# Five conversion units of 512 columns instead of eight of 320 for the lower half of w_out, and another order of the first three chunks' steps

## The chip, the cores and the metric

The kernel runs on one core of one Trainium2 chip. The metric is device time in microseconds (us) of one execution; several executions are timed and the median counts. The engines are TensorE (PE in the profile; PEld is its weight load), VectorE (DVE), ScalarE (ACT), GpSimd (POOL) and SyncE (SP, which here only issues DMAs). ACT issues a few DMAs too.

## The reference

The inputs r, k, v, w, a, b have 4 batches, 8 heads, 768 steps and 40 columns. A recurrence runs over the steps, and its output feeds a two-layer network:

```python
for t in range(S):
    y[:, :, t] = einsum('bhd,bhde->bhe', r_t, state)
    Sa = einsum('bhde,bhe->bhd', state, a_t)
    state = state * w_t[:, :, None, :] - einsum('bhd,bhe->bhde', Sa, b_t)
    state = state + einsum('bhd,bhe->bhde', v_t, k_t)
x = y.transpose(0, 2, 1, 3).reshape(3072, 320)
h = x @ w_in                                   # 320 x 2048
out = (0.5 * h * (1 + erf(h / sqrt(2)))) @ w_out   # 2048 x 320
```

The two weight matrices w_in and w_out arrive as 64-bit floats, and the kernel converts them to 32 bits itself.

## The kernel before, in words

**Chunks.** The 768 steps are cut into 12 chunks of 64. Within a chunk the recurrence is written as matrix products. For chunk c the function `logs` takes logarithms of w, `sums` builds running sums of them on PE (tiles `wT_ps` and `cum`) and takes exponentials of these on ACT. `scale_a`, `scale_b` and `scale_k` scale a, b and k by them; `turn_a`, `turn_b`, `turn_k`, `turn_v` and `turn_r` transpose on PE (eight flips of 128x128, tiles `aT_ps`, `nT_ps` and so on) and copy out of PSUM, mostly on ACT. `make_N`, `make_A`, `make_RV` and `make_M` are the products of pairs of these, each masked on DVE at L575. N must be inverted as a triangular matrix. For chunk 0 `squares` does this on PE in repeated steps (tiles `sq`, with copies on POOL, ACT and DVE between them). For later chunks `make_N` writes N to DRAM by SP (L615), `start_inverse` reads it back in another layout (L664) and solves column by column on POOL (L672, L674), `store_inverse` writes the result (L686) and `fetch_inverse` brings it back (L696, L700) as Tt. `turn_corner` transposes a part of it on DVE (tile `L`, L772), and `corner`, `joined` and `make_X` go on from there (tiles `J`, `Js`, `X`). `make_sa` and `make_saT`, `make_QY` and `outputs` end the chunk. `outputs` writes the chunk's rows of x (tile `xt`, L886, and DMAs at L894 and L897) and the next state (`st`, L906 to L909), which `turn_state` flips.

**The network.** `mlp` is a generator for one block of rows: first products `ph` at L993, the Gelu on ACT at L995, second products `po` at L1010. Each `fill()` in the order below emits one more piece of it. The xt buffer that `outputs(1)` writes is free once the `ph` of the first block is done.

**The order.** All engines run their instructions in program order, so the order in which the functions are called is the schedule. For the first three chunks the calls are written out by hand, from L1059 on; from chunk 2 on, a loop follows at L1244. `keep(n)` asks for a filler, a matmul of no use of n times 128 columns, put on PE before the next PSUM tile that `duo` hands out; when two `keep` calls meet before a tile, the last one counts. Three fillers of 512 columns stand at the very start.

**The conversion.** `to_float` converts a unit of columns: on DVE two operations on the words (L319, L321) with one on ACT (L320) after the first, then a `yield`, then three on DVE (L324, L327, L328). A variant that runs partly on POOL (L330 to L333) serves some units of w_in. `convert(1)` begins the next unit in the queue and finishes the one begun before it; `convert(0, True)` finishes what is begun. `first_load` brings raw words of w_in, `first_convert` converts them in units of 512 columns. `second_load(f, slot)` brings the raw words of rows f (128 of the 2048) of w_out by two DMAs (L401). The raw words of f = 0 to 7 lie in w_out's own SBUF memory, `late_raw`, one behind the other; those of f = 8 to 15 lie in memory that is free at the time. LW is 1024 words. `second_convert(f)` converts 320 columns.

```python
    def second_convert(f, eng):
        if wide_out:
            yield from to_float(w_out_sb[:, f], second_raw.pop(f), eng)
```

**Queues.** SP issues most DMAs in the written order, and an issue that must wait (for a landing, or for memory to come free) holds back those behind it. Rows f10 of w_out go into k's memory, so their issue waits for `scale_k(2)`. DMAs issued by ACT stand in ACT's own order of work.

Of the kernel before, what the change touches and what calls it, by code (L numbers as in the profile page):

```python
# [10 lines left out]
FP32 = mybir.dt.float32  # L11
# [8 lines left out]
def kernel(  # L20
# [71 lines left out]
    def keep(columns):  # L92

        asked[:] = [columns]
# [119 lines left out]
    def load_VR(c):  # L214
        VR = turned_in.setdefault(c, {})["VR"] = VR_ring()
        for e in range(2):
            nc.sync.dma_start(out=VR[half(e)].rearrange("p g q m d -> p (g q m) d")[:, :, :D], in_=rows_of(v, c, e))
# [188 lines left out]
    def second_convert(f, eng):  # L406
        if wide_out:
            yield from to_float(w_out_sb[:, f], second_raw.pop(f), eng)

    def first_pieces(kts, part, eng):  # L410
        queue.extend(first_convert(kt, part, eng) for kt in kts)

    def second_pieces(fs, eng):
        queue.extend(second_convert(f, eng) for f in fs)

    def run(steps):
# [6 lines left out]
    def logs(c):  # L423
        logw = raws[c, "w"][:, :G * DM]
        nc.scalar.activation(logw, logw, ACT.Ln)

    def sums(c):
        logw = raws.pop((c, "w"))
        pt = duo("wT_ps").rearrange("p e (n t) -> p e n t", t=C)
        for n in range(G * NP):  # L430
            for x in range(2):
                for e in range(2):
                    at = (2 * n + x) * D
                    mm(pt[half(x), e, n], logw[half(e), at:at + HP], cum_m[half(e), half(e)])
        cum = duo("cum")[:, :, :DM]
        for g in range(G):
            for e in range(1 if c < NB else 2):
                q = half(e ^ g) if c >= NB else slice(0, P)
                mm(cum[half(e) if c >= NB else q, g], cum_m[q, q], logw[q, g * DM:(g + 1) * DM])
        wp = wp_ring()  # L440
        turned_in.setdefault(c, {})["wp"] = wp
        if c < NB:
            nc.scalar.activation(wp[:, :, 1:].rearrange("p (n e) t -> p e n t", e=2), pt, ACT.Exp)  # L443
        else:
            en = turned_in.setdefault(c, {})["en"] = by_batch(side("en", "kT", 1))
            for to, scale_ in ((wp[:, :, 1:].rearrange("p (g n e) t -> p g e n t", g=G, e=2), 1.0),
                               (en.rearrange("p (e g n) t -> p g e n t", e=2, g=G), -1.0)):
                for g in range(G):
                    nc.scalar.activation(to[:, g], pt[:, ::1 - 2 * g, g * NP:(g + 1) * NP], ACT.Exp, scale=scale_)
        rw = (avs_ring if c in (1, 2) else part_ring)()[:, :, :DM]  # L450
        nc.scalar.activation(rw, cum, ACT.Exp, scale=-1.0)
        decays[c] = rw.rearrange("p g (h d) -> p g h d", h=H), wp
# [25 lines left out]
    def turn_a(c):  # L478
        if c < NT:
            turned_in.setdefault(c, {})["a_ps"] = flip(by_pair(raws.pop((c, "a"))), "aT_ps")  # L480
            return
        aT = turned_in.setdefault(c, {})["aT"] = work.tile([P, 2, G, NP, C], FP32, tag="aT", name="aT", bufs=2)
        turn(aT.rearrange("p e g i t -> p (e g i) t"), c, "a")
# [569 lines left out]
    def warm(*columns):  # L1053

        pt = duo("warm")
        for n, cols in enumerate(columns):
            mm(pt[:, n % 2, :cols * P], ident, cum_m.unsqueeze(1).to_broadcast([P, cols, P]))

    logs(0)  # L1059
    keep(4)  # L1060
    keep(1)
    sums(0)
    turn_a(0)
    scale_b(0)
    load_r(0)
    spare_N = work.tile([P, BL * BL], FP32, tag="Nb", name="Nb"), work.tile([P, BL // 2 * BL], FP32, tag="W", name="W")
    turn_b(0)
    load_VR(0)
    nw = BL // 2 * BL
    fetch(0, "k", k, nc.sync)  # L1070
    spare_st = st_ring()
    spare_w = spare_st.rearrange("p e i g d -> p (e i g d)")
    logs(1)
    scale_a(0)
    make_N(0)
    zero = squares(0, spare_w, *spare_N, nc.gpsimd)
    next(zero)
    sums(1)
    scale_b(1)
    turn_a(1)  # L1080
    turn_b(1)
    first_pieces((0,), 0, nc.vector)
    fetch(1, "k", k, nc.sync, ahead["k"])
    spare_x = work.tile([P, NK, TB], FP32, tag="xt", name="spare_x").rearrange("p k t -> p (k t)")
    scale_a(1)
    scale_k(0)
    make_N(1)
    next(zero)
    next(zero)
    next(zero)  # L1090
    run(start_inverse(1, nc.gpsimd, (spare_x[:, :BL * BL], spare_w[:, :nw], spare_w[:, nw:])))
# [12 lines left out]
    corner_direct(0, (nc.scalar, nc.scalar, nc.scalar, nc.scalar))  # L1104
    first_load(False, 1, eng=nc.sync)
    make_av(0)
    make_y2(0)
    turn_k(1)
    make_X(0)
    first_pieces((1, 2), 0, nc.gpsimd)  # L1110
    mask_RV(0)
    first_pieces((3,), 0, nc.vector)
    load_VR(1)
    joined_direct(0)
    load_r(1)
    make_A(1, False)
    convert(1)
    convert(0, True)
    load_a(2)
    make_sa(0)  # L1120
    convert(0, True)
    load_w(2)
    mask_A(1)
    make_saT(0)
    convert(0, True)
    convert(1)
    make_M(0)
    logs(2)
    keep(1)
    make_QY(0)  # L1130
    first_load(False, 2, early(5, 4), eng=nc.sync)
    convert(1)
    fetch(2, "b", b, nc.sync)
    first_pieces((4,), 0, nc.gpsimd)
    store_inverse(1)
    convert(0, True)
    fetch(2, "k", k, nc.sync)
    fetch_inverse(1)
    pieces.append(mlp(0))
    turn_v(1)  # L1140
    convert(1)
    first_load(False, 3, eng=nc.sync)
    outputs(0)
    corner(1)
    keep(2)
    convert(1)
    keep(4)
    first_pieces(range(NK - 1), 1, nc.gpsimd)
    make_av(1)
    first_load(True, 1, spare_raw[:, :LW], eng=nc.sync)  # L1150
    convert(0, True)
    second_load(1, 2, eng=nc.sync)
    keep(3)
    keep(1)
    make_X(1)
    sums(2)
    joined(1)
    turn_r(1)
    scale_b(2)
    spare_rT = words("rT", 2)  # L1160
    turn_state()
    convert(1)
    second_load(0, 0, eng=nc.scalar)
    turn_a(2)
    turn_b(2)
    scale_a(2)
    pieces.append(mlp(1))
    keep(4)
    make_RV(1)
    first_pieces((NK - 1,), 1, nc.vector)  # L1170
    for n in "av": unused(paired[n], nc.gpsimd)
    make_sa(1)
    keep(1)
    convert(1)
    make_N(2)
    convert(1)
    convert(1)
    fill()
    scale_k(2, nc.vector)
    run(start_inverse(2, nc.gpsimd))  # L1180
    make_saT(1)
    convert(1)
    second_load(10, 0, k_rows[0][:, :2 * DM].bitcast(UINT32), eng=nc.sync)
    convert(0, True)
    convert(0, True)
    second_load(7, 14, eng=nc.sync)
    fill()
    second_load(2, 4, eng=nc.sync)
    make_y2(1)
    second_load(4, 8, eng=nc.scalar)  # L1190
    second_load(5, 10, eng=nc.sync)
    second_load(9, 2, spare_raw, eng=nc.sync)
    load_VR(2)
    make_M(1)
    second_load(3, 6, eng=nc.scalar)
    load_r(2)
    second_pieces(range(NF), nc.vector)
    make_QY(1)
    convert(1)
    convert(1)  # L1200
    second_load(6, 12, eng=nc.scalar)
    convert(1)
    second_load(8, 0, spare_raw, eng=nc.sync)
    load_VR(3)
    convert(1)
    turn_k(2)
    second_load(11, 0, spare_rT, eng=nc.scalar)
    convert(1)
    fill()
    fill()  # L1210
    load_a(3)
    load_w(3)
# [1 line left out]
    outputs(1)  # L1214
    turn_r(2)
    turn_v(2)
    convert(1)
    logs(3)
    make_RV(2)
    make_A(2)  # L1220
    convert(1)
    fetch(3, "b", b, nc.sync)
    convert(1)
    sums(3)
    turn_a(3)
    convert(1)
    make_av(2)
    second_load(12, 12, eng=nc.sync)
    store_inverse(2)
    fetch_inverse(2)  # L1230
    convert(1)
    unused(paired["r"], nc.vector)
    convert(1)
    turn_state()
    turn_corner(2)
    convert(1)
    second_load(13, 14, eng=nc.sync)
    scale_b(3)
    scale_a(3)
    fetch(3, "k", k, nc.sync)  # L1240
    fill()
    second_load(15, 0, spare_rT, eng=nc.sync)

    for c in range(2, NCH):  # L1244
        n, n2 = c + 1, c + 2
# [122 lines left out]
```

## Time and profile before

| | |
|---|---|
| median of 6 runs | 713.01 us |
| the six runs | 710.23 to 715.96 us |
| the profiled execution | 711.44 us |
| its span, first to last instruction | 709.7 us |
| mean granted PE clock | 0.959 of full |
| busy over the span | PE 671.0, DVE 368.6, POOL 346.3, ACT 219.5 us |

Busy time is summed per engine. Lines such as L324 are lines of the kernel before. The granted clock is the share of full speed that PE is given; it is 0.5 or 1.0 at any time here, and a mean over a stretch lies between. In a timeline line, the first figure is the start, the second the duration; the bracket at the end gives the idle time of the engine just ahead and what ended it.

### The profile page before, as it was taken

The page shows a single profiled execution, that of the slowest core. Times are in us where ns is not written, and L with a number is a line of the kernel's source. Part 1 is how long each engine was busy: PE and PEld are TensorE (multiplying, and loading weights), DVE is VectorE, ACT ScalarE, POOL GpSimd, SP SyncE. Part 2 cuts the span into 40 slices and gives each one's busy share as a digit, 9 for nine tenths or more (in the row PEclk, how much of TensorE's full clock was granted, in tenths as well). Part 3 has the DMA queues.
Part 4 walks back from the last instruction along what each step waited for, and adds up shares of the span by engine and source line. Part 5 has one row for each costly group of instructions (what it writes and reads, how often), then busy time and mean ns, then how long its engine had stood idle before and what let it go on. Part 6 is the DMA issues. An engine that isn't in the chain of part 4 may idle for free.

```text
span 709.7 us, 32732 instructions
## 1 busy us (share of the span) xinstructions
PE 671.0 (95%) x14778; PEld 588.5 (83%) x14778; DVE 368.6 (52%) x485; ACT 219.5 (31%) x304; POOL 346.3 (49%) x798
## 2 busy tenths in 40 slices
PE   7778897869999999999999999999999999999997
PEld 5667787748877877899899898998998898998987
DVE  2324689994353365365484474572672772522303
ACT  5223665443140240351241332232323413112020
POOL 4375358810851842861853844826816818800000
PEclk9575799999999999999999999999999999999999
DMA  9588637763667657656656747747638563120100
GB/s 130 96 176 146 121 88 201 138 128 89 124 121 114 131 99 108 130 103 110 130 103 118 133 90 133 140 77 142 133 68 159 112 108 61 29 46 4 31 8 19
DMA packets 287923, 74.46 MB, mean 105 GB/s; under 512 B 265736, under 2 KB 284456, under 8 KB 287784
## 3 DMA queue, kind: packets, MB, share of 16 engines
q1 hardware_dynamic: 283360, 68.20, 51.5%
q0 software_dynamic: 864, 2.36, 2.1%
q8 instruction: 116, 1.90, 1.1%
q10 hardware_dynamic: 3560, 1.80, 0.9%
q14 instruction: 23, 0.19, 0.1%
HBM read 58.69 MB, written 9.70 MB: 96 GB/s over the span
## 4 chain that ended last, share of the span: by engine, by line
PE 81%; SPq 6%; DVE 5%; DMA 3%; ACT 2%; issue 2%; ACTq 1%; DVEq 0%
PE ph L993 29%; PE po L946 19%; PE po L1010 7%; PE QY L110 6%; PE J L110 2%; PE X L110 2%; PE av L110 2%; PE wT_ps L110 2%; PE RV_ps L110 2%; SPq L383 2%; PE sap L110 2%; PE N_ps L110 2%; PE saT_ps L110 1%; PE A_ps L110 1%; PE M_ps L110 1%
## 5 line engine op out<-in xcount | busy, mean ns | idle before, releaser
L993 PE MATMUL ph<-xt,w_in_sb 64*128 64x256 f32 x1920 | 219.9, 381 | 0.7 <-issue 0.7
L993 PEld LDWEIGHTS ph<-xt,w_in_sb 64*128 64x128 f32 x1920 | 183.1, 187 | 22.7 <-issue 1.6
L672 POOL TENSOR_TENSOR tmp<-W,Nb 128x126 f32<-128x126 f32 (+22 forms) x310 | 122.3, 394 | 159.9 <-DMA Nb<-N 136.9
L674 POOL TENSOR_TENSOR W<-W,tmp 128x126 f32<-128x126 f32 (+22 forms) x310 | 129.3, 417 | 24.3
L995 ACT ACTIVATE gt<-ph 128x1024 f32<-128x1024 f32 x48 | 49.1, 1023 | 152.0 <-PE ph L993 151.9
L946 PE MATMUL po<-w_out_sb,gt 128*128 128x160 f32 x576 | 82.9, 302 | 0.1
L946 PEld LDWEIGHTS po<-w_out_sb,gt 128*128 128x128 f32 x576 | 78.7, 190 | 2.2 <-DVE gt L966 0.4
L1010 PE MATMUL po<-w_out_sb,gt 128*128 128x320 f32 x192 | 55.3, 445 | 3.0 <-ACT wpT L443 3.0
L1010 PEld LDWEIGHTS po<-w_out_sb,gt 128*128 128x128 f32 x192 | 36.5, 194 | 18.4 <-ACT wpT L443 3.2
L802 DVE COPY Tt<-J 32x512 f32<-32x512 f32 x11 | 7.6, 689 | 57.1 <-ACT Tt L802 57.0
L786 ACT COPY Js<-J 128x256 f32<-128x256 f32 x11 | 4.1, 370 | 94.8 <-PE J L110 94.8
L186 DVE STREAM_TRANSPOSE aT<-a_pairs 128x1024 f32<-128x1024 f32 x9 | 11.2, 1245 | 38.7 <-DMA a_pairs<-in_a_dram 38.7
L998 DVE TENSOR_TENSOR half<-gt 128x1024 f32<-128x1024 f32 x9 | 11.2, 1249 | 34.6 <-ACT gt L995 34.6
L950 DVE TENSOR_TENSOR os<-os,po 128x160 f32<-128x160 f32 x36 | 11.5, 320 | 31.2 <-PE po L946 25.5
L946 PE MATMUL po<-extra,half 128*128 128x160 f32 x176 | 26.1, 303 | 0.0
L320 ACT ACTIVATE conv<-conv,rebias 128x320 uint32<-128x320 uint32 (+1 forms) x26 | 16.2, 625 | 31.1 <-DVE conv L319 29.1
L575 DVE TENSOR_TENSOR SM<-M_ps,upper 128x1024 f32<-128x1024 f32 x12 | 14.6, 1214 | 21.4 <-PE M_ps L110 21.4
L946 PEld LDWEIGHTS po<-extra,half 128*128 128x128 f32 x176 | 24.2, 190 | 0.3
L995 ACT ACT_TABLE_LOAD x10 | 12.8, 1283 | 37.1 <-PE ph L993 37.1
L662 POOL MEMSET W<- 128x512 f32 x10 | 5.3, 529 | 32.9 <-DMA inv<-W 32.9
L886 DVE TENSOR_TENSOR xt<-QY,wpT 128x512 f32<-128x512 f32 x24 | 15.5, 686 | 10.9 <-PE QY L110 10.7
L946 PE MATMUL po<-extra,gt 128*128 128x160 f32 x144 | 21.0, 299 | 0.0
(223 smaller groups left out, 1136.8 us busy)
## 6 DMA issues: line engine op xcount, KB each, us to landing
Nb<-N SPq DMA_DIRECT2D x20, 256.0 KB
VR<-in_v_dram SPq DMA_DIRECT2D x24, 160.0 KB
out_dram<-os SPq DMA_DIRECT2D x48, 80.0 KB
b_rows<-in_b_dram SPq DMA_DIRECT2D x22, 160.0 KB
k_rows<-in_k_dram SPq DMA_DIRECT2D x22, 160.0 KB
N<-N SPq DMA_DIRECT2D x44, 64.0 KB
Tt<-inv SPq DMA_DIRECT2D x44, 64.0 KB
a_pairs<-in_a_dram SPq DMA_DIRECT2D x18, 144.0 KB
```

What stands on the lines that cost most here:

```text
L110: nc.tensor.matmul(o, lhsT, rhs, start=first, stop=True, skip_group_check=True)
L320: nc.scalar.activation(power, power, ACT.Relu, bias=rebias, scale=8.0)
L383: eng.dma_start(out=words[half(x), :n, m:m + 2 * P], in_=whole_rows[:HP, :, m:m + 2 * P])
L575: nc.vector.tensor_tensor(to, pt, upper.unsqueeze(1).to_broadcast([P, 2 * G * NP, C]), ALU.mult)
L672: eng.tensor_tensor(t, W[:, :rows, j:j + 1].to_broadcast([P, rows, rest]), Nb[:, j:j + 1, j + 1:].to_broadcast([P, rows, rest]), ALU.mult)
L674: eng.tensor_tensor(W[:, :rows, j + 1:], W[:, :rows, j + 1:], t, ALU.add)
L886: nc.vector.tensor_tensor(xt[:, :NP, g * P:(g + 1) * P].rearrange("p i (e t) -> p i e t", e=2), Y, wp[:, g, :, :, :C], ALU.mult)
L946: nc.tensor.matmul(po[:, n, :DM // 2], l_[:, f], r_[:, f], start=f == 0, stop=f == NF // 2 - 1)
L950: nc.vector.tensor_tensor(to, one_, other, ALU.add)
L993: nc.tensor.matmul(ph[:, x, s], w_in_sb[half(x), kt, p * P:(p + 1) * P], xt[half(x), kt], start=kt == 0, stop=kt == NK - 1)
L995: nc.scalar.activation(gt[:, 4 * q:4 * q + 4].rearrange("p (x s) t -> p x s t", x=2), ph, ACT.Gelu)
L1010: nc.tensor.matmul(po[:, g], gt[:, f, g * P:(g + 1) * P], w_out_sb[:, f], start=f == 0, stop=f == NF - 1)
```

## The change

It has two parts. In the first, rows f = 0 to 7 of w_out, whose raw words lie one behind the other, are converted by a new function `second_wide(u)` in five units of 512 columns (NK is 5, and one unit covers LW = 1024 raw words), instead of eight of 320; the rows f = 8 to 15 remain units of 320. Unit 0 needs the loads f0 and f1, unit 1 needs f1, f2 and f3, unit 2 f3 and f4, unit 3 f4, f5 and f6, unit 4 f6 and f7. In all there are 13 units instead of 16, and so 65 DVE operations and 13 on ACT instead of 80 and 16. The loads f12 and f13 go into the raw memory of rows 6 and 7, so they now stand behind unit 4.

In the second, the calls of the first three chunks are in another order. On the engines that comes to this. On PE the fillers are 512 columns before nT(0), nT(1), vT(1), av(1) and aT(2) and 128 before sap(1); they were 128 before wT(0) and vT(1), 512 before av(1), 128 before X(1), 512 before RV(1) and 128 before N(2). The flips nT(0) come ahead of aT(0), and A(2) ahead of RV(2). On SP the fetch of k for chunk 1 stands behind the write of N(1); f2, f5 and f4 stand ahead of f10, and f7 after f8; the store of inv(2) stands ahead of f12. f4 goes from ACT's queue to SP, f9 and f15 from SP to ACT's queue (f9 ahead of f3). On DVE the pieces of units stand elsewhere between the masks of chunks 1 and 2, and scale_a(3) comes ahead of scale_b(3). POOL's order stays. The diff (in the changed kernel, lines from L410 on are 5 or 6 higher):

```diff
--- before.py
+++ after.py
@@ -407,10 +407,16 @@
         if wide_out:
             yield from to_float(w_out_sb[:, f], second_raw.pop(f), eng)
 
+    def second_wide(u, eng):
+        if wide_out:
+            at = slice(u * LW // 2, (u + 1) * LW // 2)
+            yield from to_float(w_out_sb.rearrange("p f d -> p (f d)")[:, at], late_raw[:, u * LW:(u + 1) * LW], eng)
+
     def first_pieces(kts, part, eng):
         queue.extend(first_convert(kt, part, eng) for kt in kts)
 
     def second_pieces(fs, eng):
+        queue.extend(second_wide(u, eng) for u in range(NK))
         queue.extend(second_convert(f, eng) for f in fs)
 
     def run(steps):
@@ -1056,36 +1062,36 @@
         for n, cols in enumerate(columns):
             mm(pt[:, n % 2, :cols * P], ident, cum_m.unsqueeze(1).to_broadcast([P, cols, P]))
 
+    nw = BL // 2 * BL
     logs(0)
+    sums(0)
+    spare_N = work.tile([P, BL * BL], FP32, tag="Nb", name="Nb"), work.tile([P, BL // 2 * BL], FP32, tag="W", name="W")
     keep(4)
-    keep(1)
-    sums(0)
-    turn_a(0)
     scale_b(0)
     load_r(0)
-    spare_N = work.tile([P, BL * BL], FP32, tag="Nb", name="Nb"), work.tile([P, BL // 2 * BL], FP32, tag="W", name="W")
+    load_VR(0)
+    fetch(0, "k", k, nc.sync)
     turn_b(0)
-    load_VR(0)
-    nw = BL // 2 * BL
-    fetch(0, "k", k, nc.sync)
+    turn_a(0)
+    scale_a(0)
     spare_st = st_ring()
     spare_w = spare_st.rearrange("p e i g d -> p (e i g d)")
+    zero = squares(0, spare_w, *spare_N, nc.gpsimd)
+    make_N(0)
     logs(1)
-    scale_a(0)
-    make_N(0)
-    zero = squares(0, spare_w, *spare_N, nc.gpsimd)
     next(zero)
     sums(1)
     scale_b(1)
+    first_pieces((0,), 0, nc.vector)
     turn_a(1)
+    keep(4)
     turn_b(1)
-    first_pieces((0,), 0, nc.vector)
-    fetch(1, "k", k, nc.sync, ahead["k"])
     spare_x = work.tile([P, NK, TB], FP32, tag="xt", name="spare_x").rearrange("p k t -> p (k t)")
     scale_a(1)
     scale_k(0)
     make_N(1)
     next(zero)
+    fetch(1, "k", k, nc.sync, ahead["k"])
     next(zero)
     next(zero)
     run(start_inverse(1, nc.gpsimd, (spare_x[:, :BL * BL], spare_w[:, :nw], spare_w[:, nw:])))
@@ -1104,109 +1110,103 @@
     corner_direct(0, (nc.scalar, nc.scalar, nc.scalar, nc.scalar))
     first_load(False, 1, eng=nc.sync)
     make_av(0)
+    turn_k(1)
+    first_pieces((1, 2), 0, nc.gpsimd)
     make_y2(0)
-    turn_k(1)
+    mask_RV(0)
     make_X(0)
-    first_pieces((1, 2), 0, nc.gpsimd)
-    mask_RV(0)
+    load_VR(1)
+    load_r(1)
+    load_a(2)
     first_pieces((3,), 0, nc.vector)
-    load_VR(1)
     joined_direct(0)
-    load_r(1)
     make_A(1, False)
     convert(1)
     convert(0, True)
-    load_a(2)
-    make_sa(0)
     convert(0, True)
     load_w(2)
+    convert(0, True)
     mask_A(1)
+    make_sa(0)
     make_saT(0)
-    convert(0, True)
     convert(1)
     make_M(0)
     logs(2)
-    keep(1)
+    first_load(False, 2, early(5, 4), eng=nc.sync)
+    first_pieces((4,), 0, nc.gpsimd)
     make_QY(0)
-    first_load(False, 2, early(5, 4), eng=nc.sync)
     convert(1)
     fetch(2, "b", b, nc.sync)
-    first_pieces((4,), 0, nc.gpsimd)
     store_inverse(1)
     convert(0, True)
+    keep(4)
     fetch(2, "k", k, nc.sync)
     fetch_inverse(1)
+    convert(1)
+    first_load(False, 3, eng=nc.sync)
+    outputs(0)
+    first_load(True, 1, spare_raw[:, :LW], eng=nc.sync)
     pieces.append(mlp(0))
     turn_v(1)
-    convert(1)
-    first_load(False, 3, eng=nc.sync)
-    outputs(0)
     corner(1)
-    keep(2)
     convert(1)
     keep(4)
     first_pieces(range(NK - 1), 1, nc.gpsimd)
+    convert(0, True)
     make_av(1)
-    first_load(True, 1, spare_raw[:, :LW], eng=nc.sync)
-    convert(0, True)
     second_load(1, 2, eng=nc.sync)
-    keep(3)
-    keep(1)
     make_X(1)
     sums(2)
     joined(1)
+    spare_rT = words("rT", 2)
     turn_r(1)
+    turn_state()
+    keep(4)
     scale_b(2)
-    spare_rT = words("rT", 2)
-    turn_state()
-    convert(1)
-    second_load(0, 0, eng=nc.scalar)
+    convert(1)
     turn_a(2)
+    pieces.append(mlp(1))
     turn_b(2)
     scale_a(2)
-    pieces.append(mlp(1))
-    keep(4)
+    second_load(0, 0, eng=nc.scalar)
     make_RV(1)
     first_pieces((NK - 1,), 1, nc.vector)
+    keep(1)
     for n in "av": unused(paired[n], nc.gpsimd)
     make_sa(1)
-    keep(1)
     convert(1)
     make_N(2)
     convert(1)
+    convert(0, True)
     convert(1)
     fill()
     scale_k(2, nc.vector)
     run(start_inverse(2, nc.gpsimd))
     make_saT(1)
     convert(1)
+    fill()
+    make_y2(1)
+    second_load(2, 4, eng=nc.sync)
+    second_load(5, 10, eng=nc.sync)
+    second_load(4, 8, eng=nc.sync)
     second_load(10, 0, k_rows[0][:, :2 * DM].bitcast(UINT32), eng=nc.sync)
     convert(0, True)
-    convert(0, True)
+    load_VR(2)
+    second_load(9, 2, spare_raw, eng=nc.scalar)
+    second_load(3, 6, eng=nc.scalar)
+    make_M(1)
+    load_r(2)
+    second_pieces(range(NF // 2, NF), nc.vector)
+    make_QY(1)
+    convert(1)
+    second_load(6, 12, eng=nc.scalar)
+    turn_k(2)
+    load_VR(3)
+    second_load(8, 0, spare_raw, eng=nc.sync)
+    convert(1)
+    fill()
+    convert(1)
     second_load(7, 14, eng=nc.sync)
-    fill()
-    second_load(2, 4, eng=nc.sync)
-    make_y2(1)
-    second_load(4, 8, eng=nc.scalar)
-    second_load(5, 10, eng=nc.sync)
-    second_load(9, 2, spare_raw, eng=nc.sync)
-    load_VR(2)
-    make_M(1)
-    second_load(3, 6, eng=nc.scalar)
-    load_r(2)
-    second_pieces(range(NF), nc.vector)
-    make_QY(1)
-    convert(1)
-    convert(1)
-    second_load(6, 12, eng=nc.scalar)
-    convert(1)
-    second_load(8, 0, spare_raw, eng=nc.sync)
-    load_VR(3)
-    convert(1)
-    turn_k(2)
-    second_load(11, 0, spare_rT, eng=nc.scalar)
-    convert(1)
-    fill()
     fill()
     load_a(3)
     load_w(3)
@@ -1214,32 +1214,32 @@
     outputs(1)
     turn_r(2)
     turn_v(2)
-    convert(1)
+    second_load(11, 0, spare_rT, eng=nc.scalar)
     logs(3)
+    make_A(2)
+    convert(1)
+    fetch(3, "b", b, nc.sync)
     make_RV(2)
-    make_A(2)
-    convert(1)
-    fetch(3, "b", b, nc.sync)
-    convert(1)
+    convert(1)
+    unused(paired["r"], nc.vector)
+    store_inverse(2)
     sums(3)
     turn_a(3)
+    second_load(12, 12, eng=nc.sync)
     convert(1)
     make_av(2)
-    second_load(12, 12, eng=nc.sync)
-    store_inverse(2)
     fetch_inverse(2)
     convert(1)
-    unused(paired["r"], nc.vector)
-    convert(1)
+    convert(1)
+    turn_corner(2)
+    convert(1)
+    scale_a(3)
+    second_load(15, 0, spare_rT, eng=nc.scalar)
+    second_load(13, 14, eng=nc.sync)
     turn_state()
-    turn_corner(2)
-    convert(1)
-    second_load(13, 14, eng=nc.sync)
-    scale_b(3)
-    scale_a(3)
     fetch(3, "k", k, nc.sync)
     fill()
-    second_load(15, 0, spare_rT, eng=nc.sync)
+    scale_b(3)
 
     for c in range(2, NCH):
         n, n2 = c + 1, c + 2
```

More of the change, by code (lines that the diff above doesn't have):

```diff
@@ L1128 @@
     logs(2)
-    keep(1)
+    first_load(False, 2, early(5, 4), eng=nc.sync)
+    first_pieces((4,), 0, nc.gpsimd)
     make_QY(0)
-    first_load(False, 2, early(5, 4), eng=nc.sync)
     convert(1)
     fetch(2, "b", b, nc.sync)
-    first_pieces((4,), 0, nc.gpsimd)
     store_inverse(1)
     convert(0, True)
+    keep(4)
     fetch(2, "k", k, nc.sync)
     fetch_inverse(1)
-    pieces.append(mlp(0))
-    turn_v(1)
     convert(1)
@@ L1143 @@
     outputs(0)
+    first_load(True, 1, spare_raw[:, :LW], eng=nc.sync)
+    pieces.append(mlp(0))
+    turn_v(1)
     corner(1)
-    keep(2)
     convert(1)
@@ L1182 @@
     convert(1)
+    fill()
[3 more added lines that the diff above has]
+    second_load(4, 8, eng=nc.sync)
     second_load(10, 0, k_rows[0][:, :2 * DM].bitcast(UINT32), eng=nc.sync)
     convert(0, True)
-    convert(0, True)
-    second_load(7, 14, eng=nc.sync)
-    fill()
-    second_load(2, 4, eng=nc.sync)
-    make_y2(1)
-    second_load(4, 8, eng=nc.scalar)
-    second_load(5, 10, eng=nc.sync)
-    second_load(9, 2, spare_raw, eng=nc.sync)
     load_VR(2)
+    second_load(9, 2, spare_raw, eng=nc.scalar)
+    second_load(3, 6, eng=nc.scalar)
     make_M(1)
-    second_load(3, 6, eng=nc.scalar)
     load_r(2)
-    second_pieces(range(NF), nc.vector)
+    second_pieces(range(NF // 2, NF), nc.vector)
     make_QY(1)
     convert(1)
-    convert(1)
     second_load(6, 12, eng=nc.scalar)
-    convert(1)
+    turn_k(2)
+    load_VR(3)
     second_load(8, 0, spare_raw, eng=nc.sync)
-    load_VR(3)
-    convert(1)
-    turn_k(2)
-    second_load(11, 0, spare_rT, eng=nc.scalar)
     convert(1)
     fill()
+    convert(1)
+    second_load(7, 14, eng=nc.sync)
     fill()
@@ L1216 @@
     turn_v(2)
-    convert(1)
+    second_load(11, 0, spare_rT, eng=nc.scalar)
     logs(3)
-    make_RV(2)
     make_A(2)
@@ L1222 @@
     fetch(3, "b", b, nc.sync)
+    make_RV(2)
     convert(1)
+    unused(paired["r"], nc.vector)
+    store_inverse(2)
     sums(3)
     turn_a(3)
+    second_load(12, 12, eng=nc.sync)
     convert(1)
     make_av(2)
-    second_load(12, 12, eng=nc.sync)
-    store_inverse(2)
     fetch_inverse(2)
     convert(1)
-    unused(paired["r"], nc.vector)
     convert(1)
-    turn_state()
     turn_corner(2)
     convert(1)
+    scale_a(3)
+    second_load(15, 0, spare_rT, eng=nc.scalar)
     second_load(13, 14, eng=nc.sync)
-    scale_b(3)
-    scale_a(3)
+    turn_state()
     fetch(3, "k", k, nc.sync)
     fill()
-    second_load(15, 0, spare_rT, eng=nc.sync)
+    scale_b(3)
     for c in range(2, NCH):
```

## The prediction

> **What bounds the kernel now.** I read the page's forty slices first, then windows by stage, then windows on the grid on which the granted clock changes, then the timeline at three places. In the slices:
> ```profile
> PE   7778897869999999999999999999999999999997
> PEclk9575799999999999999999999999999999999999
> ```
> Each digit is 17.7 us. TensorE (PE) is full from the tenth slice on; in the second to the fifth it runs far below full clock, and in those its busy digits (7, 7, 8, 8) hold work that would be shorter at full clock. The stages (us, then busy time of PE, weight load, DVE, ACT, POOL with counts, clock, DMA share, GB/s):
> ```profile
> 0.00:52.00 52.00, 38.81 (x984) 31.04 (x984) 14.71 (x17) 17.68 (x20) 26.72 (x75) 0.77 0.79 135
> 52.00:79.32 27.32, 22.52 (x660) 20.52 (x664) 13.85 (x20) 12.87 (x20) 13.36 (x31) 0.50 0.83 143
> 98.50:116.60 18.10, 13.68 (x337) 11.81 (x336) 17.47 (x20) 10.59 (x15) 15.47 (x21) 1.00 0.53 142
> 116.60:131.20 14.60, 14.59 (x217) 13.11 (x217) 14.11 (x27) 4.73 (x7) 12.48 (x28) 0.88 0.98 210
> 131.20:152.30 21.10, 14.20 (x326) 11.02 (x324) 20.41 (x41) 12.95 (x17) 12.28 (x32) 1.00 0.63 112
> 164.90:709.70 544.80, 538.09 (x11396) 477.41 (x11392) 264.52 (x325) 145.86 (x204) 258.43 (x608) 1.00 0.52 96
> ```
> After 164.9 PE idles 6.7 us of 544.8 and the diff has no work there: only an earlier start of that stage can shorten it. Until 52 PE waits on chains through other engines, partly at half clock; from 98.5 to 116.6 and from 131.2 to 152.3 DVE is full; between those, PE. The clock changes on a grid of 3.41 us:
> ```profile
> 11.05:14.46 3.41, 1.84 (x50) 1.47 (x52) 1.61 (x2) 1.66 (x2) 0.00 (x0) 1.00 1.16 153
> 21.29:24.70 3.41, 1.50 (x12) 1.05 (x10) 2.49 (x2) 0.75 (x1) 2.21 (x2) 1.00 0.76 118
> 24.70:28.12 3.42, 3.11 (x150) 2.99 (x154) 1.05 (x1) 0.26 (x1) 0.00 (x0) 0.50 0.02 5
> 41.77:45.18 3.41, 2.31 (x84) 2.22 (x85) 1.06 (x2) 1.01 (x1) 2.83 (x8) 1.00 0.49 113
> 62.25:65.66 3.41, 3.41 (x107) 3.02 (x109) 0.34 (x1) 2.20 (x4) 2.17 (x9) 0.50 1.08 231
> 144.17:147.58 3.41, 1.88 (x7) 1.41 (x8) 3.34 (x8) 3.08 (x5) 0.65 (x2) 1.00 1.18 221
> ```
> A full-clock window with 1.84 or 1.50 us of PE work is followed by half clock; one with 1.88 keeps it. The way up is less plain: 62.25 to 65.66 is full and no rise follows.
>
> **Fillers and the front.** Before, the fillers in the front are one of 128 columns at wT(0) and one at vT(1) (0.49 us). After, there are 512-column ones ahead of nT(0), nT(1) and vT(1), each 1.13 us at full clock like the one at av(1). The chain of chunk 1 in the timeline:
> ```profile
> 20.34 0.70 ACT L451 ACTIVATE avs<-cum 128x640 f32<-128x640 f32 x1 [1.37 <-PE cum L110]
> 21.08 1.56 DVE L489 SCALAR_TENSOR_TENSOR extra<-early_b,avs 128x640 f32<-128x640 f32 x1 [3.16 <-ACT avs L451]
> 22.79 1.06 PE L459 MATMUL nT_ps<-ident,extra 128*128 128x128 f32 x8 [1.07 <-DVE extra L489]
> 25.01 1.99 PE L110 MATMUL N_ps<-aT,nT 40*64 40x64 f32 x64 [1.16 <-ACT nT L523]
> ```
> PE waits 1.07 us before nT(1), so a filler of 1.13 costs at most 0.1 there, and lifts 21.29–24.70 from 1.50 to about 2.5 busy, above the 1.88 that kept the clock. Then N(1) takes about 1.16 us, as products of this shape do at full clock, not 1.99; the first squaring 1.2 instead of 2.00, the second (128 products, 3.64) about 1.9: 0.8 + 0.8 + 1.7 = 3.3 us at most, and 1.7 if only the first two lie on the path. The filler at nT(0) falls in PE's wait for scale_b(0) (0.47 us idle ahead of nT(0), 0.21 ahead of aT(0), which now comes second); it makes N(0) up to 0.5 later, and its 1.13 with the flips behind it shift: I put nT(0) at 11.2, aT(0) at 12.1 to 13.1, N(0) at 14.4. In 11.05–14.46 then lie the two flips of 1.06 and 1.07 whole, less the 0.15 of nT(0) that starts ahead: 1.97, for 1.84 now. If that keeps the clock at 14.46, wT(1) (1.98) and cum(1) (2.50) halve too and N(1) starts some 2.7 earlier: 6.1 in all. I take 4, between 1.7 and 6.1, nearer the middle because a margin of 0.09 over 1.88 is thin.
>
> [...]
>
> **Front queues.** fetch(1,"k") (two DMAs, 1.75 us of SP) goes behind N(1)'s write. SP, freed, then waits for N's landing in any case; behind it queues only the issue of the inverse's columns (0.48 us) and the loads of w_in. Its 320 KB may land beside those columns and delay them by 0 to 2 us; the inverse has about 4 us to spare before L(1) at 82.77. Zero, to +0.5.
>
> **Middle.** At vT(1) the filler grows by 0.64, those at X(1) (0.49) and RV(1) go: between -0.3 and +0.5, taken as 0. PE is busy 18.47 of the 19.18 us from 79.32 to 98.50, so none of it is hidden. A filler before sap(1) lies in DVE-bound time. SP before is stuck behind f10 until 110.71; after, f2, f5, f4 are ahead of it, so they land earlier. f3 stays on ACT's queue, behind f9 now: +1 us, landing near 118.9 against 117.96.
>
> **Conversion.** A unit is five DVE operations and one on ACT:
> ```profile
> L324 DVE SCALAR_TENSOR_TENSOR conv<-words,conv 128x320 uint32<-128x320 uint32 x2 | 1.0, 484 | 0.0
> L324 DVE SCALAR_TENSOR_TENSOR conv<-w_out_sb,conv 128x512 uint32<-128x512 uint32 x5 | 3.4, 691 | 3.3 <-ACT conv L320 3.3
> ```
> Each column costs 1.08 ns, the rest is fixed, near 0.14 us. Undisturbed, 320 columns take 0.32 + 0.32 + 0.48 + 0.48 + 0.49 = 2.09; 512 take 0.42 + 0.42 + 0.69 + 0.74 + 0.69 = 2.96. Eight by 2.09 less five by 2.96: 16.7 - 14.8 = 1.9 us of DVE; beside POOL's chain, where L324 averages 638 ns, up to 4. ACT loses 8 × 0.56 - 5 × 0.73 = 0.8. How much counts? Up to 131.2 PE has 14.59 of 14.60 busy, and outputs(1) waits for it:
> ```profile
> 131.26 1.29 DVE L886 TENSOR_TENSOR xt<-QY,wpT 128x512 f32<-128x512 f32 x2 [0.24 <-PE ph L993]
> 152.33 0.71 DVE L772 STREAM_TRANSPOSE L<-Tt 128x512 f32<-128x512 f32 x1
> 153.19 0.74 PE L110 MATMUL J<-L,N 32*32 32x32 f32 x64 [2.92 <-DVE L L772]
> ```
> So units 0 to 2 save nothing by themselves, and their new wait (unit 1 needs f1, f2 and f3) costs nothing: a stall of some 1.5 us for f3 ends unit 2 near 128.2, 3 us before 131.2. Queued behind that wait on DVE are unit 0's finish and outputs(1); beyond 121.8 the stall becomes time. Between outputs(1) and L(2) DVE now does six starts and six finishes of units of 320 (0.32 + 0.32 and 0.48 + 0.48 + 0.49 undisturbed: 12.5 us in all); after, five starts (one of 512) and five finishes (two of 512): 0.84 + 4 × 0.64 + 2 × 2.12 + 3 × 1.45 = 12.0. That is -0.5 undisturbed, -1.0 with the sharing above; the masks, transposes and the clearing of r beside them are the same. L(2) also needs the inverse, whose chain on POOL (113.06 to 144.9) is 31.8 us here against 27.6 for chunk 1, partly from sharing with DVE; fewer DVE operations shorten it by 0 to 1.5, and its store (145.14) no longer queues behind f12's load. I count 0.5 in all. If the inverse is late, L(2) stays where it is and the 0.5 is gone. In scale_a(3), scale_b(3) swapped, scale_b ends 1.2 later, under second products of the first block that keep PE full to 161.1; f15 on ACT's queue delays the state's copy to about 157.5, under the same cover. Gone, these are +1.2 at most.
>
> **Sum.** -4 (front) + 0 (middle) - 0.5 = -4.5. The profiled run took 711.44 with a span of 709.7, 1.6 below the median of 713.01. So 707 on that run's footing, 708.5 as a median.
>
> **Rivals.** *Only the conversion counts* (0.30): the clock falls in the same windows or N(1)'s lead is lost in chunk 0's chain, which shares the same engines. For it: 1.97 against 1.88, and POOL's 26.72 of work before 52. Then -1 to 0: 712.5.
>
> *The rise at 41.77 is lost* (0.20, slower): the work that raised the clock there is chunk 0's 128-wide k flips, which straddle that boundary if the front moves by 1 to 3 us. From 41.77 to 52.0 PE has 2.31 + 3.42 + 1.13 = 6.9 us at full clock, which at half cost 6.9 more; less 3.4 in front: +3.5, 716.5. It decides from the point where the flips end before the boundary and the following windows see only small products, as at 62.25. Against it: a front that is earlier by a whole window also brings the flips into the window before, and the rise with them.
>
> *A late f3 stalls DVE* (0.05, within the range of the others): with f3 landing 5 us later than I put it, unit 1 starts at 124, unit 2 ends near 133.2, outputs(1) and L(2) are 2 us late, and 2 of the front's 4 are gone: about 711.
>
> **Numbers.** The forecast has 0.45, spread over 703.5 to 711 by the front's 1.7 to 6.1 and the middle's bounds; conversion only 0.30; lost rise 0.20; late f3 0.05. 0.5% is 3.6 us, about what a measurement tells from no change: 709.4 and 716.6. Below 709.4 lie 0.36 of the forecast and 0.04 of the second case, whose ends spread by a run or two either way. A lost rise without the gain in front gives 713.0 + 6.9 = 719.9, with it 716.5: 0.15 of its 0.20 lies above 716.6, and 0.05 more comes from a late f3 together with a late inverse. The rest, 0.40, is between. Range 703.5 to 717.
>
> **What would show it.** Right: N(1) ends by 24 at 1.2 us, the granted clock near 1.00 over 14 to 31, L(2) about 4 to 5 before 152.33, and the stage from J(2) on unchanged at 544.8 or so. Wrong: a clock still 0.50 from 24.7; half clock between 41 and 52; unit 1's first step on DVE after 121.8; L(2) waiting for the inverse and not for DVE.

## The result, and the profile after

| | before | changed |
|---|---|---|
| median | 713.06 us (79 runs) | 716.85 us (37 runs) |
| lowest to highest | 707.46 to 721.31 | 712.06 to 721.18 |
| profiled execution, its span | 711.44, 709.7 | 716.72, 715.0 |
| mean granted clock in it | 0.959 | 0.954 |

The ratio is 1.0051, with an interval of 1.0039 to 1.0063: the changed kernel is slower by about half a per cent, some 3.8 us. The forecast was 708.5. The ratios and intervals in this text leave out three runs in a slower state of the chip (one each of e1, e3 and e6 below), while the medians keep them, so that a ratio need not be that of the medians beside it.

I read the profile after in the order of the one before. In the line of the granted clock over forty slices there is less half clock in the front, a little in the seventh slice, and more in the ninth and tenth (143 to 179 us), where before all are 9:

```profile
PEclk9775698978999999999999999999999999999999
```

The stages, cut at the same times as before (us, then busy time of PE, weight load, DVE, ACT, POOL with counts, clock, DMA share, GB/s):

```profile
0.00:52.00 52.00, 36.80 (x984) 28.00 (x984) 14.88 (x17) 17.68 (x20) 24.05 (x69) 0.87 0.81 126
116.60:131.20 14.60, 12.26 (x192) 11.36 (x194) 10.78 (x17) 3.69 (x5) 12.64 (x26) 0.77 0.90 188
131.20:152.30 21.10, 18.75 (x352) 14.64 (x348) 19.21 (x33) 11.64 (x15) 16.09 (x35) 0.92 0.53 104
152.30:164.90 12.60, 7.71 (x138) 5.96 (x139) 9.89 (x22) 2.97 (x5) 0.77 (x3) 0.59 0.69 142
```

Up to 52 us PE does the same 984 instructions in 2 us less busy time, at a mean clock of 0.87 for 0.77. Still nothing behind them is earlier. In the last stretch PE is busy 7.71 of 12.60 us, at a clock of 0.59. The same stretch before, with 10.61 us busy at 0.86:

```profile
152.30:164.90 12.60, 10.61 (x282) 8.39 (x282) 8.81 (x18) 2.39 (x4) 0.00 (x0) 0.86 0.47 112
```

A ledger by landmarks of the two timelines, the start of each step, before and after: N(1) 25.01 and 26.23; L(1) 82.77 and 85.06; L(2) 152.33 and 156.34; N(3) 163.09 and 168.78; the product sap(2) 169.55 and 175.59. So the changed kernel is 2.3 later at L(1), loses 1.7 from there to L(2), 1.7 from L(2) to N(3) and 0.3 to sap(2). From sap(2) to the end it takes 539.4 us against 540.2. That adds up to the 5.3 us between the spans.

The first 2.3 of these can't be put down to the change. Three executions have before's order up to there, before itself and e1 and e6 below: they start L(1) at 82.77, 84.67 and 82.34. Two executions of the changed kernel, this one and e12 below, start it at 85.06 and 81.50. What is left is around L(2). In the timeline there:

```profile
156.34 0.71 DVE L778 STREAM_TRANSPOSE L<-Tt 128x512 f32<-128x512 f32 x1 [1.26 <-DMA Tt<-inv]
157.19 1.08 PE L110 MATMUL J<-L,N 32*32 32x32 f32 x64 [5.26 <-DVE L L778]
158.20 1.95 PE L110 MATMUL X<-st,aT 40*64 40x40 f32 x64
```

Before, DVE was busy right up to L(2); now it has nothing left to do and waits 1.26 us for the inverse (Tt). PE waits 5.26 us for J instead of 2.92, its granted clock is 0.50 from 154.22 on, and X(2) takes 1.95 us; in e9 below, at full clock, it is 1.14.

### The profile page after: what moved, and what is told of

The parts are those of the page before. It is cut to its first block, busy times and chain, and to the rows that moved or that the text cites. A ratio compares the mean times of both kernels' runs of the same rounds, so it can differ in the third digit from the quotient of the medians.

```text
span 715.0 us, 32719 instructions
## 1 busy us (share of the span) xinstructions
PE 673.6 (94%) x14778; PEld 588.9 (82%) x14778; DVE 365.8 (51%) x470; ACT 219.2 (31%) x301; POOL 347.7 (49%) x798
## 3 DMA queue, kind: packets, MB, share of 16 engines
q0 software_dynamic: 864, 2.36, 2.1%
## 4 chain that ended last, share of the span: by engine, by line
PE 81%; POOL 6%; issue 3%; DVE 2%; SPq 2%; DMA 2%; ACT 2%; ACTq 1%; DVEq 0%; POOLq 0%
PE ph L999 28%; PE po L952 19%; PE po L1016 7%; PE QY L110 5%; PE J L110 2%; POOL W L680 2%; POOL tmp L678 2%; PE RV_ps L110 2%; PE sq L110 2%; PE sap L110 2%; PE X L110 2%; PE N_ps L110 2%; PE saT_ps L110 1%; PE av L110 1%; PE A_ps L110 1%
## 5 line engine op out<-in xcount | busy, mean ns | idle before, releaser
L678 POOL TENSOR_TENSOR tmp<-W,Nb 128x126 f32<-128x126 f32 (+22 forms) x310 | 124.5, 402 | 162.6 <-DMA Nb<-N 139.6
L1001 ACT ACTIVATE gt<-ph 128x1024 f32<-128x1024 f32 x48 | 49.1, 1024 | 154.6 <-PE ph L999 154.5
L320 ACT ACTIVATE conv<-conv,rebias 128x512 uint32<-128x512 uint32 (+1 forms) x23 | 15.2, 666 | 25.2 <-DVE conv L319 25.1
```

The lines of the kernel that those rows point to most:

```text
L320: nc.scalar.activation(power, power, ACT.Relu, bias=rebias, scale=8.0)
L678: eng.tensor_tensor(t, W[:, :rows, j:j + 1].to_broadcast([P, rows, rest]), Nb[:, j:j + 1, j + 1:].to_broadcast([P, rows, rest]), ALU.mult)
L1001: nc.scalar.activation(gt[:, 4 * q:4 * q + 4].rearrange("p (x s) t -> p x s t", x=2), ph, ACT.Gelu)
```

## The experiments

There are two theories. **F**, the front: the new order of the front costs time, because PE there waits for its own instruction code, as I read the 2.38 us at cum(1) in which PE is idle and the profile shows no wait. **W**, the width: the longer DVE operations of the wide units hold up POOL, which works on the inverse of chunk 2 at that time, and the inverse is late. In what follows, "chain" is POOL's work on that inverse, from its first to its last column.

**e1_wide_only**: before, with the units of the changed kernel in the old order.

```diff
-    second_pieces(range(NF), nc.vector)
+    second_pieces(range(NF // 2, NF), nc.vector)   # and second_wide for u = 0..4; three convert(1) fewer
```

> The kernel before in its own order, but rows 0 to 7 of w_out converted in five units of 512 (three convert calls fewer). Theory F (front): the loss of the changed kernel comes from the new order of the front, where PE then waits for its own instruction code (2.4 us at cum(1), 2.0 at a squaring); the wide units by themselves save a little: 711.5 to 713, L(2) at 152.3 or up to 1 us earlier. Rival W (wide units): the longer DVE operations disturb POOL's inverse of chunk 2 (34.6 us long in the changed kernel, 31.8 before), L(2) then waits for the inverse and PE falls to half clock: 714.5 to 716, chain on POOL over 33 us.

Measured: 718.5 us against 714.37 for before on the same chip, ratio 1.0032 (1.0001 to 1.0063). Chain 35.2 us, L(2) waits 2.04 us for the inverse. This is what W expects; the ratio makes 2.3 us, and its interval lies only just clear of no change.

**e2_order_only**: the changed order with eight units of 320.

```diff
-        queue.extend(second_wide(u, eng) for u in range(NK))
-    second_pieces(range(NF // 2, NF), nc.vector)
+    second_pieces(range(NF), nc.vector)            # and three convert(1) more
```

> The changed kernel's order, with rows 0 to 7 of w_out in eight units of 320 as before (three more convert calls). Theory F: as slow as the changed kernel, 716 to 718. Rival W: most of the loss is gone, 713 to 714.5, and POOL's chain for chunk 2 is back near 32 us.

Measured: 0.9989 (0.9960 to 1.0018). Chain 31.4 us, no wait for the inverse, PE waits 0.96 us for J. This speaks for W.

**e3_old_front** and **e4_new_front**: the lines from the first `sums(0)` to the start of chunk 1's inverse exchanged: e3 is the changed kernel with the old lines (the diff shows their start), e4 the kernel before with the new ones.

```diff
-    sums(0)
-    keep(4)
-    scale_b(0)
+    keep(4)
+    keep(1)
+    sums(0)
+    turn_a(0)
+    scale_b(0)
...
```

> The changed kernel with the front (from the first sums to the start of chunk 1's inverse) in the order of before, with its fillers; everything behind as changed. Theory F: N(1) at 25.0, squaring and RV(0) 1.5 us earlier than in the changed kernel, L(1) near 82.8 instead of 85.1; 713 to 714.5. Rival W: L(1) earlier, but the later loss (some 3 us between 116 and 165) stays: 715 to 716.

> The kernel before with only the front in the changed order, with its fillers. Theory F: 714.5 to 716.5, L(1) near 85. Rival W: 713 to 714.

Measured: e3 1.0003 (0.9973 to 1.0032), chain 34.5, L(2) waits 1.39; e4 1.0003 (0.9975 to 1.0031), chain 31.9, L(2) waits 1.11. e3 is better than W alone allows, though its trace shows W's wait, and its L(1) is at 85.67, where F had expected 82.8. e4 is better than F allows; and its L(2) waits for the inverse with narrow units and a chain of 31.9, so width is not the only source of that wait. Width isn't everything in the changed kernel, then, and the front alone costs too little to be seen.

By now the effect on POOL could be read from six traces. In the changed kernel, a POOL operation over 108 columns beside two wide DVE operations:

```profile
140.91 0.73 POOL L678 TENSOR_TENSOR tmp<-W,Nb 128x108 f32<-128x108 f32 x1
141.31 0.88 DVE L327 SCALAR_TENSOR_TENSOR conv<-w_out_sb,conv 128x512 f32<-128x512 uint32 x1
141.72 0.73 POOL L680 TENSOR_TENSOR W<-W,tmp 128x108 f32<-128x108 f32 x1
```

The same POOL operation in the kernel before, beside the same line of a unit of 320:

```profile
136.34 0.69 DVE L327 SCALAR_TENSOR_TENSOR conv<-w_out_sb,conv 128x320 f32<-128x320 uint32 x1
136.76 0.53 POOL L672 TENSOR_TENSOR tmp<-W,Nb 128x108 f32<-128x108 f32 x1
```

It takes 0.73 instead of 0.53 us. The next runs add or remove this by itself.

**e5_wide_cut**: the changed kernel, each of L324, L327 and L328 of a wide unit in two halves.

```diff
-        eng.scalar_tensor_tensor(dst, mant_f, 2.0 ** -20, power_f, ALU.mult, ALU.mult)
+        for s in at:    # two slices of 256 columns; L324 and L327 in the same way
+            eng.scalar_tensor_tensor(dst[:, s], mant_f[:, s], 2.0 ** -20, power_f[:, s], ALU.mult, ALU.mult)
```

> The changed kernel, but in the five wide units each of the last three DVE operations (L324, L327, L328) is cut in two halves of 256 columns: 15 more DVE instructions, some 2 us more DVE time in all, the same data and order. Theory W (long DVE operations hold up POOL: in the first four runs and the two profiles before, a POOL operation beside L327 or L328 took 0.13 to 0.15 us more at 320 columns and 0.34 more at 512, and the chain for chunk 2 lasted 31.4 to 31.9 us with narrow units and 34.5 to 35.2 with wide ones): the chain is back to 31 to 32 us, and the time falls to 0.998 to 1.002 of before in spite of more DVE work. Rival D (the loss sits in DVE's own order or in the front): 1.005 to 1.008, the chain no matter.

Measured: 1.0017 (0.9996 to 1.0037). Chain 31.4 us, no wait of L(2) for the inverse. Chain and wait are as W expects. In time, with 15 more DVE instructions, the kernel is below the changed one's 1.0051 (1.0039 to 1.0063); but that was measured at another time, and e12 below gives the changed kernel 1.0022, so the cut is judged by e9 and e10.

**e6_late_chain**: before, and the inverse alone made late.

```diff
-        eng.memset(W, 0.0)
+        for _ in range(1 + extra):    # extra is 6 for chunk 2
+            eng.memset(W, 0.0)
```

> The kernel before, narrow units, with six more clears of W (0.52 us each) on POOL ahead of chunk 2's inverse, which so ends some 3 us later and is otherwise as it was. If the lateness of the inverse is what the wide units cost: 1.002 to 1.005, with L(2) starting on the arrival of the inverse. If the inverse has slack and the wide units cost something else: 0.999 to 1.001.

Measured: 1.0015 (0.9991 to 1.0039), not clear of no change. The 1.002 to 1.005 expected of a costly late inverse was missed. In the trace L(2) waits, but for much less than with the wide units:

```profile
154.33 0.71 DVE L773 STREAM_TRANSPOSE L<-Tt 128x512 f32<-128x512 f32 x1 [0.27 <-DMA Tt<-inv]
155.19 0.74 PE L110 MATMUL J<-L,N 32*32 32x32 f32 x64 [3.83 <-DVE L L773]
```

L(2) waits 0.27 us for the inverse, PE waits 3.83 us for J, and X(2) behind J takes 1.95 us, at half clock.

**e7_a_flips_first** and **e8_a_first_k_early**: e2 with the a flips first and the filler between the flips cut from 512 to 256 columns; e8 has also the fetch of k back in its place.

```diff
+    turn_a(0)
-    keep(4)
+    keep(2)
     scale_b(0)
...
     turn_b(0)
-    turn_a(0)
     scale_a(0)
```

> The changed order with narrow units (as in e2_order_only), but the flips aT(0) again ahead of nT(0), and the filler between them 256 columns instead of 512. Theory F (PE's wait of 2.4 us for its code at cum(1) comes from N(0) starting 0.9 us later, at 14.8): N(0) back at 13.8 to 13.9, the code lands by 16, N(1) at 22.5 to 23.5 instead of 26.2; what reaches the end is -0.5 to -3 us against e2_order_only, so 0.995 to 0.999 of before. Rival (the code is late whatever PE does, or the front is absorbed later): N(1) at 25 to 26, or no change in time, 0.998 to 1.000.

> As e7_a_flips_first, with the fetch of chunk 1's k also back ahead of N(1)'s write. Chain of chunk 1 on POOL starts at 35 to 37 instead of 39.7. If that chain has slack, no difference to e7 (within 0.1%); if it has none, 1 to 2 us less than e7.

Measured: e7 0.9981 (0.9958 to 1.0005), N(1) at 24.62; e8 0.9992 (0.9970 to 1.0015), N(1) at 22.91. The idle time at cum(1) is gone in e7 and 0.22 us in e8. In e7 the clock was at half during cum(1), which took 2.50 us, so N(1) missed the expected 22.5 to 23.5. Neither time is clear of e2's 0.9989. Moving the fetch of k made no difference that can be seen.

The last four were measured together, on one chip. **e9_cut_a_first** is e5 with e7's front, **e10_wide_a_first** the changed kernel with e7's front, **e11_narrow_cut** is e7 with the last three operations of each unit of 320 in halves of 160, and **e12_changed_again** the changed kernel.

> e5_wide_cut (the changed kernel with the last three DVE operations of each wide unit in halves of 256) with the front of e7_a_flips_first. If the wait of DVE for the inverse was the main cost of the change and the front costs 0.1%: 0.997 to 1.000 of before, chain for chunk 2 near 31.5 us, no wait of L(2) for the inverse. If the units still cost something when cut: 1.001 to 1.003.

> The changed kernel, wide units uncut, with only the front of e7_a_flips_first: N(1) near 24.6 instead of 26.2. If the wide units are the main cause, the chain is still 34.5 us or longer, L(2) waits 1 to 2 us for the inverse, and the time is 1.003 to 1.005. If the front's wait for code is the main cause: 1.000 to 1.002.

> e7_a_flips_first with the last three DVE operations of each of the eight units of 320 cut in halves of 160: 24 more DVE instructions, 3.4 us more DVE time by 0.14 us each. If a POOL operation waits longer the longer the DVE operation beside it, it takes about 0.05 us more beside 160 columns (0.14 beside 320, 0.34 beside 512) and the chain is 30 to 31 us; as DVE is then the later of the two at L(2), the time is 0.2 to 0.5% above e7: 1.000 to 1.003. If it is not length that matters, the chain stays at 31.5.

> The changed kernel itself, on the chip and in the call of the three above, for the comparison: 1.004 to 1.006 by every theory; L(2) waits 1 to 2 us for the inverse, PE 5 us for J.

| | ratio to before | interval | median, us | chain, us | L(2) waits for the inverse | PE waits for J |
|---|---|---|---|---|---|---|
| e9 | 0.9976 | 0.9956 to 0.9997 | 711.29 | 31.3 | no | 0.99 |
| e10 | 1.0008 | 0.9989 to 1.0027 | 714.00 | 34.6 | 1.61 | 5.76 |
| e11 | 1.0019 | 0.9996 to 1.0041 | 714.76 | 28.7 | no | 2.84 |
| e12 | 1.0022 | 0.9999 to 1.0045 | 715.39 | 34.7 | 1.21 | 5.19 |

Before, measured with them, had a median of 712.56. e9 beats both kernels: cut units, a flips first, and the rest of the new order. e9 and e10 differ only in the cut, and by 2.7 us in their medians; from the twelve times of each the means differ by 2.1 us, with an interval of about 0.7 to 3.4. This is the cleanest price of the uncut wide units on record. e10 and e12 differ only in the front, by 1.4 us in their medians, which is not clear of nothing. e12 missed what every theory expected: it is less slow here than the changed kernel was over its 37 runs. And e10 splits the expectations: chain and wait are W's, but its time is below the 1.003 that W gives and within what was expected if the front's wait were the main cause. e11 shows the other side of length: the chain is the shortest of all, but DVE has 24 more instructions and is now the late one.

In e9 the same steps as shown above:

```profile
152.89 0.71 DVE L782 STREAM_TRANSPOSE L<-Tt 128x512 f32<-128x512 f32 x1
153.75 0.83 PE L110 MATMUL J<-L,N 32*32 32x32 f32 x64 [0.99 <-DVE L L782]
154.51 1.14 PE L110 MATMUL X<-st,aT 40*64 40x40 f32 x64
```

No wait on L(2), 0.99 us on J, X(2) at full clock. In e11, beside DVE operations of 160 columns (two in one line of the view), the POOL operation over 108 columns:

```profile
133.78 1.03 DVE L330 SCALAR_TENSOR_TENSOR conv<-w_out_sb,conv 128x160 f32<-128x160 uint32 x2
134.23 0.40 POOL L683 TENSOR_TENSOR W<-W,tmp 128x108 f32<-128x108 f32 x1
```

So 0.73 beside 512 columns, 0.53 beside 320, 0.40 beside 160.

## Why the prediction was wrong, point by point

**Two terms of the sum failed.** The forecast was -4 from the front and -0.5 from the conversion; measured was +3.8. The front's 4 us were the larger miss: by e4, which has the new front alone, they are +0.2 us (-1.8 to +2.2). The conversion had the wrong sign, and is what makes the kernel slower and not merely equal: 2.3 us by e1 (0.1 to 4.5), about 2 by e9 and e10.

**The cost of the wide units had the wrong sign.** The working said that "fewer DVE operations shorten" POOL's chain "by 0 to 1.5". It counted operations and not their length. The mean excess of a POOL operation over the same one left alone, beside L327 or L328, is 0.01 us at 160 columns, 0.07 at 256, 0.13 to 0.16 at 320 and 0.33 to 0.36 at 512 (left alone, such an operation takes 0.18 us and 1.88 ns a column, a line through those with nothing beside them). Five wide units so made the chain 34.5 to 35.2 us long in five traces, against 31.3 to 31.9 in seven with units of 320 or cut in 256 (before, e2, e4, e5, e7, e8 and e9): 3 us longer, where I had a gain. The inverse reached L(2) 1.2 to 2.0 us after DVE was ready for it, in all five.

The lines differ too: at 512 columns the excess is 0.33 to 0.36 us beside L327 and L328, 0.21 to 0.23 beside L324, and 0.06 to 0.10 beside L321, which is small but not nothing. Whether that goes with their inputs in SBUF, two in L324, L327 and L328 and one in L321, was not tried. The trace of before already spoke against the change: at 114.23 a POOL operation over 30 columns takes 0.56 us beside the L327 of a unit of w_in, 512 columns wide, which is 0.33 above the line for one left alone. The prediction, which names the sharing, did not weigh it by length.

**What a late inverse costs comes through the clock.** Between L(2) and N(3) lie 11.9 to 12.6 us in the seven traces in which L(2) waits for the inverse (the changed kernel twice, e1, e3, e10, e4 and e6), and 9.15 to 10.85 in the other seven. That this is the clock is read from X(2): 1.95 us in six of the seven (1.65 in e4), 1.14 to 1.53 in the others. In the changed kernel the granted clock is 0.50 from 154.22 to 164.46, in before from 154.40 to 157.82. In the seven, PE waits 3.5 to 5.8 us for J, in the others 0.96 to 3.74. So the stretch gets up to 3 us longer. That does not always reach the end: e4 and e6 have narrow units and the same 12.4 us from L(2) to N(3), with waits of L(2) of 1.11 and 0.27 us, and their times, 1.0003 and 1.0015, are not clear of no change. The runs don't show why.

**The front's 4 us were not there.** In the first window the clock did what that step said. This is the window that the prediction put at 1.97, and the one after the gain:

```profile
11.05:14.46 3.41, 1.94 (x16) 1.73 (x16) 1.22 (x2) 1.98 (x2) 0.00 (x0) 1.00 1.46 154
17.88:21.29 3.41, 1.57 (x9) 1.29 (x10) 0.62 (x1) 0.56 (x2) 3.18 (x4) 0.97 0.92 121
```

Behind the window with 1.94 busy the clock stayed full: it was 1.00 in 14.46 to 17.88, wT(1) took 1.14 us instead of 1.98, and then PE stopped in cum(1):

```profile
19.71 1.07 PE L110 MATMUL cum<-SM,cum_m 128*128 128x320 f32 x3 [2.38 <-issue]
21.87 1.91 PE L110 MATMUL nT_ps<-cum_m,ident 128*128 128x512 f32 x2
23.57 1.50 PE L465 MATMUL nT_ps<-ident,extra 128*128 128x128 f32 x8
26.23 1.16 PE L110 MATMUL N_ps<-aT,nT 40*64 40x64 f32 x64 [1.16 <-ACT nT L529]
```

"issue" is idle time for which the profile shows no wait. The transfers of the instruction queue suggest what it was: a block of 16,384 bytes ran from 16.49 to 18.07, and PE went on 1.6 us after it. In before that block had landed by 15.76, and PE, at half clock, came to the place at 17.8. So my reading is that a faster PE ran into the end of its code. That the block holds PE's code is inferred: the trace doesn't name its engine, but in all nine traces with idle time at this place (0.22 to 2.71 us) PE goes on 1.5 to 1.75 us after the block has landed. The same wait, 2.3 to 2.7 us, is in all five traces with this front, and 1.38 in e6, whose old front happened to run at full clock. The window with the wait had 1.57 us busy, the clock behind it was 0.53 (21.29 to 24.70), and the filler meant for PE's idle time ran at half clock, 1.91 us. So the front's term left out a wait that in these traces PE meets only when it is faster.

Nor is the border that the prediction drew, between 1.84 and 1.88 us of work, a border. In e1 a full-clock window with 1.62 keeps the clock, in e3 one with 2.36 is followed by half clock:

```profile
20.93:24.35 3.42, 1.62 (x13) 1.18 (x11) 2.88 (x2) 0.34 (x2) 2.03 (x2) 1.00 0.94 156
24.35:27.76 3.41, 1.81 (x124) 1.64 (x128) 1.23 (x1) 0.68 (x1) 0.61 (x1) 1.00 0.02 5
137.67:141.08 3.41, 2.36 (x130) 2.05 (x128) 2.51 (x5) 3.02 (x4) 2.86 (x8) 1.00 0.56 152
141.08:144.49 3.41, 3.34 (x67) 2.83 (x68) 3.38 (x5) 0.63 (x2) 3.02 (x6) 0.50 0.14 30
```

So the margin of 0.09, on which the 4 us rested, was none; what decides is open.

With the a flips ahead of nT(0), N(0) starts at 13.2 to 13.8 (e7 to e11) instead of 13.8 to 14.8, and the wait is 0.8 us or less; the trace of e10:

```profile
17.40 1.07 PE L110 MATMUL cum<-SM,cum_m 128*128 128x320 f32 x3 [0.31 <-issue]
22.91 1.16 PE L110 MATMUL N_ps<-aT,nT 40*64 40x64 f32 x64 [1.16 <-ACT nT L529]
```

But the earlier N(1) does not reach the end: L(1) is at 82.10 in e10 and at 81.50 in e12, whose N(1) is 2 us later. Over all traces L(1) is at 82.3 to 85.7 with the old front (four), 81.5 to 85.5 with the changed one (five) and 81.3 to 83.7 with the a flips first (five). Where between them the lead is lost was not followed. Taking away most of this wait is worth 1.4 us in the medians (e12 less e10), which is not clear of nothing. The second case of the prediction had said as much ("N(1)'s lead is lost in chunk 0's chain").

**The stall before unit 1 was as forecast, what followed it was not.** Unit 1 began at 121.09 after a wait of 1.44 us for its load, within the 121.8 I had set. But unit 2 did not end near 128.2: it ended at 134.0, as the conversions then waited 1.49 and 1.04 us for ACT's part of them (L320), which stands behind the copy of k's flips and the Gelus on ACT. The 3 us of slack ahead of outputs(1) were used up; but they cost nothing there, as the first products that outputs(1) waits for ended on PE at 134.07.

**The rivals.** In the changed kernel the clock did rise, at 41.58 (0.50 in the 3.41 us before, 1.00 up to 51.82), so the slower case that I priced is not what happened. Its time, 716.5, was near the measured one by luck: no rival had a longer chain on POOL. **Right** were the stage behind (sap(2) to the end within 0.8 us), and the sign to look for, "L(2) waiting for the inverse and not for DVE". The range, 703.5 to 717, held the median, at its edge, and by that same luck.

**What stays open.** e3 (1.0003) has the wide units and the wait, and is not slower than before; in a sum of effects it should be near 1.003. The changed kernel's own ratio is 1.0051 over its 37 runs and 1.0022 in e12, so sets of runs differ by about that much, but this isn't shown to be the cause. The steps in the traces don't settle it either: from L(1) to sap(2) the five kernels with uncut wide units take 90.0 to 91.6 us, and the nine others 86.8 to 91.3, with e2, e7 and e11 at 91 though no inverse was late in them. So the longer chain and the wait on it are shown, and that the uncut units cost some 2 us; of the 3.8 us the rest has no shown cause. If PE did wait for code, whether that came late because it was asked for later or because the transfer stood behind others was not tried.

## What to carry to other kernels

Fewer, longer instructions were a gain here only on the engine that ran them: before joining operations on one engine, ask which engine slows down beside it and whether that one carries a chain with a due time. Cutting the wide operations in two (256 columns) gave the chain its time back, but gave up the gain on DVE, which is busy 368.6 us in e9 as in the kernel before, against 365.8 in the changed one. And a saving in front of PE is worth little while landmarks move by 2 to 3.6 us between executions of the same instructions (L(1) at 82.34 to 84.67 and at 81.50 and 85.06): take a step's price from several executions, and from the stage whose wait ends last.

## What the runs showed of the hardware that I had not expected

- A POOL operation's delay grew here much faster than the length of the DVE operation beside it (L327 and L328): 0.01, 0.07, 0.14 and 0.34 us beside 160, 256, 320 and 512 columns.
- PE waited up to 2.7 us with nothing that the profile shows to wait for, and resumed 1.5 to 1.75 us after a block of 16,384 bytes had landed (nine traces; that the block held PE's code is inferred).
- How much PE work a full-clock window held did not decide whether the clock stayed: behind one with 1.62 us it was 1.00 (e1), behind one with 2.36 us 0.50 (e3).
